# Narrowing 64-bit weights with one VectorE pass fewer and one ScalarE pass more, a group begun in halves, and new dates for a written schedule

## The chip, the cores and the metric

The kernel runs on one core of a Trainium2 chip. The metric is the device time of one execution in microseconds (us). Five engines work side by side, each in the order of its own queue: TensorE (PE in the profile), VectorE (DVE), ScalarE (ACT), GpSimd (POOL) and SyncE (SP), which here only starts DMAs. They wait for each other through semaphores.

## The reference

Two layers follow each other. The first is a recurrence over time with a complex decay, the second a gated feed-forward layer.

```python
# q, k, v, a_re, a_im: (4 batches, 8 heads, 768 steps, 48), float32
mag = sqrt(a_re * a_re + a_im * a_im)
scale = minimum(mag, 0.999) / (mag + 1e-06)
a_re_n, a_im_n = a_re * scale, a_im * scale
for t in range(S):
    new_re = ar * S_re - ai * S_im          # S: 48 x 48 for each batch and head
    new_im = ar * S_im + ai * S_re
    S_re, S_im = new_re + outer(k[t], v[t]), new_im
    y[t] = q[t] @ S_re
# x = y as (3072 tokens, 384); weights 384 x 1536, 384 x 1536, 1536 x 384
rms = sqrt(mean(x * x, axis=-1) + 1e-06)
xn = x / rms * rms_g
g = xn @ w_gate
out = (g * sigmoid(g) * (xn @ w_val)) @ w_out
```

The inputs of the first layer and `rms_g` are float32. The three weight matrices are divided by a square root from NumPy, and so they arrive as float64.

## The kernel before, in words

**Chunks, units and groups.** The 3072 tokens are cut into 24 chunks of 128 steps (`n`), six to a batch. `gates(u)` works out the decays of a unit: units 0 and 1 hold one chunk each, every later one holds two. Its stages are named "size", "root", "turn" and "rot": squares, roots and running products of the magnitudes, running sums of the angles, sines of them, and at the end q and k turned and scaled (`rot0`, `rot1`, `kin`). Six DMAs then lay the turned rows out for TensorE (`kq0`, `kq1`). `send_decays` sends the decay at the end of a chunk to the state: for units 0 and 1 by a small product on TensorE out of `ot1` and `ot0`, for the others by DMA. `attend(n)` makes the masked score products (`kq`, masked into `am` by VectorE), the outputs `y` in bank 6, the new state through bank 5 (`vn`, `kt`), and the norm: squares (`sq`), a column sum on TensorE (`ones`), `ssv` on VectorE, a power of -0.5 on GpSimd (`rs`), and that scale spread over 128 rows by a product with `ident`. The normed chunk goes to its half of `xT`. Two chunks are a group (`g`) for the feed-forward layer. Groups 0 to 2 are done by `feed`: six blocks `b`, each with two gate products of 256 columns into one bank and two value products into another, a Silu on ScalarE (`sg`), a product on VectorE (`hT`), and then the products with `wo`. Later groups go through `joint`, which shares products between forms of `x` and of the weights.

**The weights.** `pieces` cuts the float64 weights into twelve: pieces 0, 2 and 4 are the three thirds of `wg`, 1, 3 and 5 those of `wv` (1536 numbers to a partition each), and 6 to 11 are sixths of `wo` (768 numbers). `fetch` loads a piece by a DMA on GpSimd's queue into the room of `wo` or `hT`; a load waits for the one two pieces before it, seen by a copy of one element (`junk`), and piece 4 also for a copy (`seen`) of `kq1`. `narrow` then makes float32 out of the two words of each number. ScalarE scales the low word to its three top bits. VectorE shifts the high word left by three, puts sign and exponent right by a second pass, and adds the low bits by a third. The same weights are loaded once more later and looked at for numbers out of range (`look`); those loads are on SyncE's queue.

**The order.** Nothing is issued in the order of the code. Every call adds an operation to `Flow`, with an assumed duration, what it reads and writes (`box` gives the bytes), and a due time that follows from those that need it. `flow.shift` moves the due times of a stage by some microseconds. `schedule` picks for each engine the operation that is due first among those whose inputs it takes to be ready, by its own durations, and takes a DMA's time from its bytes and packets. `issue` then writes the instructions in that order. So a change of a duration or of a due time moves instructions on all engines. All instructions come from `issue` and therefore carry one line, L715 before and L716 after the change. `flow.warm` puts products that nobody reads (`bank3` out of `rot0`) where the planner expects TensorE to be idle early on.

## Time and profile before

| | us |
|---|---|
| median of three runs | 701.25 |
| lowest and highest of them | 699.18, 704.5 |
| the profiled execution | 701.28 |
| its span, first to last instruction | 699.5 |
| TensorE busy | 657.1 (94%) |
| VectorE busy | 559.4 (80%) |
| ScalarE busy | 477.9 (68%) |
| GpSimd busy | 59.7 (9%) |

The profiled execution is within 0.1 us of the median. Its span leaves 1.8 us outside the instructions. TensorE is nearly always busy, except at the beginning: its busy share in the first two of 40 slices of the span (17.5 us each) is 0 and 0.6, and part of that is products that nobody reads. The mean granted clock of TensorE is 0.989 of full speed.

Busy time of an engine is an average; what a change is worth has to be read at the place where the engine that sets the end waits. Since all of the kernel's instructions have one line number, groups are told apart by the names of their tiles and by their shapes.

### The profile page before, as it was taken

Reading aid. Unit: us, or ns where it says so; the run is one execution under the profiler, and the core shown is the slowest. Engines: PE = TensorE matmul, PEld = TensorE weight load, DVE = VectorE, ACT = ScalarE, POOL = GpSimd, SP = SyncE. Lnnn points to the kernel's source line nnn. Section 1 sums busy time; section 2 is a strip of 40 time slices with the busy share of each in tenths; the row PEclk is TensorE's granted clock in tenths of the full one; section 3 lists DMA queues with packets and bytes.
Section 4 is the critical chain, followed back from the end, with each engine's and each line's share of the span. In section 5 each row is a group of like instructions: output and inputs, shape, how many; then the busy total and the mean of one; then the engine's idle time right before and its main releaser. Section 6 shows DMA issues by size and latency. Waiting matters only on the chain.

```text
span 699.5 us, 18714 instructions
## 1 busy us (share of the span) xinstructions
PE 657.1 (94%) x7792; PEld 607.5 (87%) x7792; DVE 559.4 (80%) x1017; ACT 477.9 (68%) x807; POOL 59.7 (9%) x108
## 2 busy tenths in 40 slices
PE   0698999999999999999999999999999998999995
PEld 0587867886889999998999999999999998999995
DVE  8989888869888788888788889888898896356462
ACT  8657777898654675574675684675674884688884
POOL 3122100011000001000101010001000010000000
PEclk9989999999999999999999999999999999999999
DMA  9995462535424243434504334424623543834422
GB/s 292 291 290 178 154 166 75 148 65 106 111 57 103 60 82 62 134 77 86 128 17 80 96 70 96 126 60 86 133 53 75 119 97 112 250 94 145 149 72 91
DMA packets 104012, 81.98 MB, mean 117 GB/s; under 512 B 41936, under 2 KB 94416, under 8 KB 103920
## 3 DMA queue, kind: packets, MB, share of 16 engines
q1 hardware_dynamic: 98560, 64.78, 34.6%
q0 software_dynamic: 4416, 15.35, 10.3%
q8 instruction: 62, 1.02, 0.6%
q10 hardware_dynamic: 944, 0.59, 0.3%
q14 instruction: 30, 0.25, 0.1%
HBM read 55.84 MB, written 4.72 MB: 87 GB/s over the span
## 4 chain that ended last, share of the span: by engine, by line
PE 79%; DVE 7%; ACT 6%; DMA 3%; SPq 2%; issue 2%; POOL 0%; DVEq 0%; ACTq 0%
PE bank L715 79%; SPq L715 2%; DMA kq<-kin 2%; ACT turns L715 2%; ACT L715 1%; DVE hT L715 1%; DVE rot L715 1%; ACT t L715 1%; DVE wv L715 1%; DVE turns L715 1%; DMA in<-in_a_im_dram 1%; DVE wg L715 1%; DMA in<-in_a_re_dram 1%; DVE t L715 1%; DVE in L715 0%
## 5 line engine op out<-in xcount | busy, mean ns | idle before, releaser
L715 PE MATMUL bank<-wo,hT 128*128 128x192 f32 (+1 forms) x696 | 143.7, 352 | 0.9 <-DVE hT L715 0.9
L715 PEld LDWEIGHTS bank<-wo,hT 128*128 128x128 f32 x696 | 115.5, 191 | 13.3 <-DVE hT L715 1.8
L715 PE MATMUL bank<-xT,wg 128*128 128x128 f32 (+1 forms) x504 | 98.2, 330 | 0.0
L715 PE MATMUL bank<-xT,wv 128*128 128x128 f32 (+1 forms) x504 | 94.3, 321 | 0.0
L715 PEld LDWEIGHTS bank<-xT,wg 128*128 128x128 f32 x504 | 80.2, 194 | 7.4 <-issue 0.4
L715 PEld LDWEIGHTS bank<-xT,wv 128*128 128x128 f32 x504 | 79.1, 192 | 5.9 <-ACT turns L715 0.2
L715 ACT ACT_TABLE_LOAD x51 | 65.4, 1283 | 7.3 <-DVE t L715 2.8
L715 ACT ACTIVATE hT<-bank 128x512 f32<-128x512 f32 x90 | 52.4, 594 | 25.9 <-PE bank L715 23.1
L715 POOL TENSOR_TENSOR rs<-ssv,mhalf 128x1 f32<-128x1 f32 x24 | 20.6, 858 | 479.0 <-DVE ssv L715 428.3
L715 ACT ACTIVATE sg<-bank 128x512 f32<-128x512 f32 (+1 forms) x72 | 38.9, 540 | 21.1 <-PE bank L715 17.9
L715 DVE TENSOR_TENSOR hT<-hT 128x768 f32<-128x768 f32 (+1 forms) x58 | 50.5, 871 | 1.1
L715 ACT ACTIVATE bank<-bank 128x512 f32<-128x512 f32 x54 | 31.5, 583 | 26.8 <-PE bank L715 18.9
L715 ACT ACTIVATE kt<-bank 128x384 f32<-128x384 f32 x40 | 19.5, 489 | 43.9 <-PE bank L715 34.8
L715 DVE COPY_PREDICATED am<-causal,bank 128x512 f32<-128x512 int32 x48 | 34.7, 731 | 16.0 <-PE bank L715 15.9
L715 PE MATMUL bank<-yg,wg 128*128 128x128 f32 x288 | 45.7, 281 | 0.0
L715 PE MATMUL bank<-sums,hT 128*128 128x192 f32 x240 | 44.7, 328 | 0.1
L715 PE MATMUL bank<-yg,wv 128*128 128x128 f32 x288 | 43.9, 275 | 0.0
L715 DVE TENSOR_TENSOR hT<-bank,hT 128x512 f32<-128x512 f32 x45 | 30.9, 688 | 14.8 <-ACT bank L715 7.8
L715 PEld LDWEIGHTS bank<-kq 96*32 96x32 f32 x1536 | 31.3, 112 | 12.6 <-issue 4.5
L715 PE MATMUL bank<-kq 96*32 96x128 f32 (+3 forms) x1536 | 37.0, 240 | 5.4 <-DMA kq<-kin 3.6
L715 ACT ACTIVATE turns<-in 128x768 f32<-128x768 f32 (+1 forms) x39 | 30.4, 791 | 13.8 <-DVE kin L715 12.7
L715 PEld LDWEIGHTS bank<-sums,hT 128*128 128x128 f32 x240 | 39.3, 190 | 0.5 <-DVE yg L715 0.2
(216 smaller groups left out, 1417.4 us busy)
## 6 DMA issues: line engine op xcount, KB each, us to landing
kq<-rot SPq DMA_DIRECT2D x90, 128.0 KB, 2.5
kq<-kin SPq DMA_DIRECT2D x54, 128.0 KB, 2.7
kin<-in_q_dram SPq DMA_DIRECT2D x24, 192.0 KB, 3.2
kin<-in_k_dram SPq DMA_DIRECT2D x24, 192.0 KB, 3.4
out_dram<-ot SPq DMA_DIRECT2D x23, 192.0 KB, 2.8
in<-in_a_re_dram SPq DMA_DIRECT2D x11, 384.0 KB, 4.3
in<-in_a_im_dram SPq DMA_DIRECT2D x11, 384.0 KB, 4.2
vn<-in_v_dram SPq DMA_DIRECT2D x20, 192.0 KB, 2.6
```

Source lines behind the costliest of these rows:

```text
L715: fn(*args, **kw)
```

## The change

Six edits come together.

`narrow` does without the second VectorE pass. ScalarE now writes the low bits as a 16-bit number into the lower half of the low word, and by one more pass the sign of the number as a bfloat16 of plus or minus one into its upper half. VectorE shifts the high word and adds the low word. What comes out is half the weight. To make up for it, `gate_col` holds twice `rms_g` and `val_col` four times, the light units are scaled by `gate_col`, and `feed` doubles the outputs of the groups before the weights are scaled.

The planner's time for a byte of DMA goes from 50.3e-6 to 41e-6. In group 0, the first two blocks of `feed` are made in 128-column halves, one for each chunk. The sending of decays becomes a stage of its own, so that it can have its own date. The table of dates is a new one.

```diff
-        load = n / row * (0.006 + 50.3e-6 * row) / 16
+        load = n / row * (0.006 + 41e-6 * row) / 16
...
+    MORE = [1.0 if x.dtype == FP32 else 2.0 for x in (w_gate, w_val, w_out)]
+    act(gate_col, gcol, AF.Copy, scale=MORE[0])
+    act(val_col, gcol, AF.Copy, scale=MORE[1] * MORE[2])
...
         t = to.bitcast(I32)
-        act(lo, lo.bitcast(U32), AF.Copy, scale=2.0 ** -29)
-        step = n // 2 if i in HALVED else n
-        for f in range(0, n, step):
-            to_, lo_, hi_ = (x[:, :, f:f + step] for x in (t, lo, hi))
-            add("DVE", [(nc.vector.tensor_scalar, (),
-                         dict(out=to_, in0=hi_, scalar1=3, scalar2=None, op0=ALU.logical_shift_left))],
-                0.15 + 0.52e-3 * rows * step, [hi_], [to_])
-            stt(to_, hi_, 0x3FFFFFFF, to_, ALU.bitwise_or, ALU.bitwise_and)
-            tt(to_, to_, lo_, ALU.add)
+        low, high = (places[i].bitcast(d).rearrange("p (c f four) -> p c f four", f=n, four=4)[:, :, :, k]
+                     for d, k in ((U16, 0), (BF16, 1)))
+        act(low, lo.bitcast(U32), AF.Copy, scale=2.0 ** -29)
+        act(high, hi.bitcast(FP32), AF.Sign)
+        add("DVE", [(nc.vector.tensor_scalar, (),
+                     dict(out=t, in0=hi, scalar1=3, scalar2=None, op0=ALU.logical_shift_left))],
+            0.15 + 0.52e-3 * rows * n, [hi], [t])
+        tt(t, t, lo, ALU.add)
...
     def send_decays(u):
         ns = UNITS[u]
+        flow.stage = "decay", u
...
-                act(yg[:, j], yT[:, j], AF.Copy, scale=gcol[:, j:j + 1])
+                act(yg[:, j], yT[:, j], AF.Copy, scale=gate_col[:, j:j + 1])
...
+    SPLIT = 2
...
             for o, w_ in zip(ps, (wg, wv)):
+                if g == 0 and b < SPLIT:
+                    for t in range(2):
+                        list_ = []
+                        for i in range(2):
+                            f = b * 2 + i
+                            for d in range(ND):
+                                list_.append((o[:, i * T + t * C:i * T + (t + 1) * C],
+                                              w_[:, f // 4, d, f % 4 * P:(f % 4 + 1) * P],
+                                              xT[:, d, t * C:(t + 1) * C], d == 0, d == ND - 1))
+                        dur = 2 * ND * mm_time(C)
+                        clock[0] += dur * SPREAD
+                        mms(list_, dur, due=clock[0] - (1 - t) * dur)
+                    continue
...
-            act(ots[i], o, AF.Copy)
+            act(ots[i], o, AF.Copy, scale=MORE[2])
...
     flow.shift = {
-        ("attend", 8): 0.6, ("attend", 9): 3.8, ("attend", 11): 3.3, ("attend", 14): 1.6, ("attend", 15): -6.6,
...
+        ("attend", 11): 2.4, ("attend", 19): -0.6, ("attend", 20): -1.1, ("attend", 21): -1.7,
...
```

**What moves at the start.** The first place is VectorE's queue where the chunks 0 and 1 are turned. `rot` is the turned q and k, `wv` and `wg` with `wo` or `hT` behind the arrow are the passes of `narrow` (`TENSOR_SCALAR` the shift, `SCALAR_TENSOR_TENSOR` the pass that goes, `ISA` the add), and `ends` and `ot1` are what the small decay product of unit 1 needs. Before:

```order
L715 TENSOR_TENSOR rot0_105<-kin_100,turns_104 128x768 x2
L715 SCALAR_TENSOR_TENSOR in0_98<-turns_104 128x384
L715 TENSOR_SCALAR wv_92<-wo_93 128x1536
L715 SCALAR_TENSOR_TENSOR wv_92<-wo_93,wv_92 128x1536
L715 TENSOR_TENSOR turns_104<-turns_104,t2_102 128x2x384
L715 TENSOR_TENSOR rot1_106<-kin_100,turns_104 128x768 x2
L715 ISA wv_92<-wo_93,wv_92 128x3072
L715 TENSOR_SCALAR wg_91<-wo_93 128x1536
L715 SCALAR_TENSOR_TENSOR wg_91<-wo_93,wg_91 128x1536
L715 ISA wg_91<-wo_93,wg_91 128x3072
L715 TENSOR_TENSOR ends_83<-t4_103,t2_102 128x3
L715 TENSOR_TENSOR ot1_134<-ends_83,ot1_134 128x24
```

After, from the same place:

```order
L716 TENSOR_TENSOR rot0_107<-kin_102,turns_106 128x768 x2
L716 SCALAR_TENSOR_TENSOR in0_100<-turns_106 128x384
L716 COPY decay0_111<-bank0_65 96x8
L716 TENSOR_TENSOR ends_85<-t4_105,t2_104 128x3
L716 TENSOR_TENSOR ot1_136<-ends_85,ot1_136 128x24
L716 ISA wg_93<-wo_95,wg_93 128x3072
L716 TENSOR_TENSOR turns_106<-turns_106,t2_104 128x2x384
L716 TENSOR_TENSOR rot1_108<-kin_102,turns_106 128x768 x2
L716 COPY decay1_112<-bank1_66 96x8
L716 TENSOR_SCALAR wg_93<-hT_96 128x1536
```

`ends` and `ot1` now stand directly behind `rot0`, where two pieces of weights stood between them.

The second place is GpSimd's queue at the same time. `in_w_gate_dram` and `in_w_val_dram` are loads of weight pieces, `seen` are the copies that wait for `kq0` and `kq1`, and `rs` are the powers of the norm of chunks 0 and 1. Before:

```order
L715 DMA hT_94<-in_w_gate_dram 128x3x1024
L715 COPY junk_138<-hT_94 1x1
L715 DMA wo_93<-in_w_val_dram 128x3x1024
L715 COPY junk_138<-hT_94 1x1
L715 COPY seen_139<-kq0_107 96x1
L715 COPY junk_138<-wo_93 1x1
L715 TENSOR_TENSOR rs0_128<-ssv_127,mhalf_75 128x1
L715 COPY seen_139<-kq1_108 96x1
L715 DMA wo_93<-in_w_gate_dram 128x3x1024
L715 DMA hT_94<-in_w_out_dram 128x2x768
L715 TENSOR_TENSOR rs1_129<-ssv_127,mhalf_75 128x1
```

After:

```order
L716 DMA hT_96<-in_w_val_dram 128x3x1024
L716 COPY junk_140<-hT_96 1x1 x2
L716 COPY seen_141<-kq0_109 96x1
L716 COPY seen_141<-kq1_110 96x1
L716 DMA wo_95<-in_w_gate_dram 128x3x1024
L716 TENSOR_TENSOR rs0_130<-ssv_129,mhalf_75 128x1
L716 DMA wo_95<-in_w_val_dram 128x3x1024
L716 TENSOR_TENSOR rs1_131<-ssv_129,mhalf_75 128x1
```

The fifth weight load now stands behind the copy that sees `kq1` landed, where before it was issued ahead of both copies. A sixth load stands directly ahead of the second power.

The third place is TensorE's queue at the state of chunk 16 (`vn`, `kt`, into bank 5) and the scores of chunk 17 into the same bank (`kq0`). Before:

```order
L715 MATMUL bank3_68<-xT1_96,wg_91 128x128 x2
L715 MATMUL bank3_68<-xT1_96,wv_92 128x128 x2
L715 MATMUL bank5_70<-vn0_121,kt0_117 32x48 x24
L715 MATMUL bank5_70<-kq0_107 32x128
L715 MATMUL bank5_70<-kq0_107 32x96
```

After:

```order
L716 MATMUL bank5_70<-vn0_123,kt0_119 32x48 x24
L716 MATMUL bank4_69<-yg1_128,wg_93 128x128 x2
L716 MATMUL bank4_69<-yg1_128,wv_94 128x128 x2
L716 MATMUL bank1_66<-ve2_122,in1_101 128x128 x2
L716 MATMUL bank1_66<-ve2_122,kq1_110 128x128 x2
L716 MATMUL bank3_68<-yg0_127,wg_93 128x128 x2
L716 MATMUL bank3_68<-yg0_127,wv_94 128x128 x2
L716 MATMUL bank4_69<-xT1_98,wg_93 128x128 x2
L716 MATMUL bank4_69<-xT1_98,wv_94 128x128 x2
L716 MATMUL bank2_67<-xT1_98,wg_93 128x128 x2
```

Three more such pairs follow before the scores; before the change the scores came next after the state.

On TensorE's queue the half products of group 0 stand behind the product that spreads the norm of chunk 1 (`ident`, `rs1`), and both halves of a bank follow each other; 17 products that nobody reads stand ahead of the scores of chunk 0, where 40 did.

More of the change, by code (lines that the diff above doesn't have):

```diff
@@ L13 @@
 BF16 = mybir.dt.bfloat16
+U16 = mybir.dt.uint16
 AF = mybir.ActivationFunctionType
@@ L846, in dma @@
         op["load"] = load
-        op["packet"] = max(0.07, 0.006 + 50.3e-6 * row * (2 if eng == "POOL" and row == 2048 else 1))
+        op["packet"] = max(0.07, 0.006 + 41e-6 * row * (2 if eng == "POOL" and row == 2048 else 1))
         return op
@@ L1613, in fast @@
-        ("norm", 19): -0.1, ("norm", 20): -0.4, ("norm", 21): -1.4, ("norm", 22): -1.4, ("root", 0): -2.0,
-        ("root", 3): 21.5, ("root", 8): -10.8, ("rot", 2): -4.7, ("rot", 9): -1.1, ("scale", 0): 2.7,
-        ("size", 3): 2.2, ("size", 4): -9.6, ("size", 6): -8.3, ("size", 9): 14.4, ("size", 11): -1.5,
-        ("state", 2): -0.3, ("state", 4): -17.0, ("state", 6): -16.7, ("state", 8): -4.3, ("state", 13): -37.5,
-        ("state", 14): -11.8, ("state", 15): -8.0, ("state", 19): -14.7, ("state", 22): -0.3, ("turn", 9): 5.8,
[3 rows of a table removed]
+        ("attend", 11): 2.4, ("attend", 19): -0.6, ("attend", 20): -1.1, ("attend", 21): -1.7,
@@ new lines, in fast @@
+        ("attend", 22): -1.4, ("decay", 8): -3.5, ("decay", 9): -3.5, ("decay", 10): -1.9, ("decay", 11): -3.5,
+        ("decay", 12): -2.9, ("feed", 1): 29.9, ("feed", 2): 6.4, ("feed", 4): 11.9, ("feed", 5): 1.7,
+        ("feed", 7): 1.9, ("feed", 8): 2.1, ("feed", 9): 2.1, ("feed", 11): 2.0, ("form", 6): 3.3,
+        ("form", 7): 11.0, ("form", 8): 45.8, ("form", 9): 9.1, ("form", 10): 46.2, ("kq", 2): 6.1,
+        ("kq", 12): 13.9, ("load", 3): -24.3, ("look", 6): 48.5, ("look", 7): 26.1, ("look", 8): -0.2,
@@ new lines, in fast @@
+        ("look", 13): 60.0, ("look", 14): 66.3, ("look", 15): 61.0, ("look", 16): 18.1, ("norm", 5): 0.1,
+        ("norm", 11): 22.7, ("norm", 21): -1.3, ("root", 0): -1.9, ("root", 4): 11.3, ("root", 10): -21.1,
+        ("root", 11): 1.8, ("rot", 4): 26.8, ("rot", 5): 1.2, ("rot", 7): 30.5, ("rot", 10): 2.2,
+        ("rot", 12): -2.8, ("size", 4): -19.9, ("size", 5): -43.2, ("size", 9): 13.7, ("size", 10): -9.5,
+        ("size", 11): -7.5, ("state", 4): -13.8, ("state", 7): -42.4, ("state", 8): -2.0, ("state", 12): 9.6,
@@ L1621, in fast @@
+        ("state", 13): -16.4, ("state", 14): -7.6, ("state", 15): -8.3, ("state", 18): -8.1,
+        ("state", 19): -5.9, ("state", 20): -8.1, ("state", 21): -8.1, ("state", 22): 6.8, ("turn", 3): 9.4,
+        ("turn", 10): 0.2, ("turn", 11): -5.5, ("turn", 12): -12.8, ("w", 0): 4.7, ("w", 1): 62.1,
+        ("y", 6): -10.7, ("y", 14): 1.6, ("y", 16): -0.3, ("y", 18): 1.3, ("y", 21): -4.2, ("y", 23): -0.6,
     }
```

11 lines of the change are left out of this document (4 added, 7 removed), and 3 rows, old and new, of the table filler.

## The prediction

> **What bounds the kernel now.** First I read the busy time by stretches (us; busy and count of PE, PEld, DVE, ACT, POOL; then clock, DMA share, GB/s), for the time before and after the first real blocks of the feed-forward layer.
>
> ```profile
> 50.00:90.00 40.00, 37.42 (x216) 31.58 (x215) 36.88 (x49) 30.24 (x40) 8.09 (x12) 0.96 0.59 185
> 60.00:693.00 633.00, 624.58 (x7366) 577.89 (x7365) 505.11 (x933) 437.50 (x744) 42.87 (x67) 1.00 0.41 101
> ```
>
> From 60 us to the last product TensorE is busy 624.58 of 633.0 us. So from there on the kernel is TensorE's work, and only 8.4 us in it are idle. No edit takes TensorE's work away. What can be won is an earlier start of that work, and parts of the 8.4. So I asked next whom TensorE waits for (us in total, times, longest), and then for its queue in the first 60 us.
>
> ```profile
> PE bank L715 <- DVE ot L715: 20.0, 2, 17.0
> PE bank L715 <- DMA kq<-kin: 3.8, 3, 2.5
> PE bank L715 <- POOL rs L715: 2.9, 2, 2.3
> PE bank L715 <- DMA kq<-rot: 1.1, 1, 1.1
> PE bank L715 <- DVE state L715: 0.7, 1, 0.7
> PE bank L715 <- DMA vn<-in_v_dram: 0.4, 1, 0.4
> ```
>
> ```profile
> 22.32 10.09 PE L715 MATMUL bank<-rot 128*128 128x128 f32 x76 [4.24 <-DVE rot L715]
> 35.47 1.13 PE L715 MATMUL bank<-ot,ot 128*96 128x8 f32 x6 [3.06 <-DVE ot L715]
> 37.59 2.36 PE L715 MATMUL bank<-kq 96*32 96x128 f32 x64
> 42.66 0.85 PE L715 MATMUL bank<-vn,kt 128*32 128x48 f32 x48
> 44.83 1.33 PE L715 MATMUL bank<-kq 96*32 96x128 f32 x64
> 54.75 0.49 PE L715 MATMUL bank<-ident,rs 128*128 128x128 f32 x2 [2.25 <-POOL rs L715]
> 55.88 4.52 PE L715 MATMUL bank<-xT,wg 128*128 128x256 f32 x12
> 60.24 2.75 PE L715 MATMUL bank<-xT,wv 128*128 128x256 f32 x12
> 62.83 2.75 PE L715 MATMUL bank<-xT,wg 128*128 128x256 f32 x12
> 93.58 1.33 PE L715 MATMUL bank<-kq 96*32 96x128 f32 x64 [1.10 <-DMA kq<-rot]
> ```
>
> The scores of chunk 0 begin at 37.59, behind the decay product of unit 1, which waited for `ot` until 35.47. Group 0 begins at 55.88. VectorE tells why `ot` is late:
>
> ```profile
> 21.31 1.83 DVE L715 TENSOR_TENSOR rot<-kin,turns 128x768 f32<-128x768 f32 x2
> 24.51 1.76 DVE L715 SCALAR_TENSOR_TENSOR wv<-wo,wv 128x1536 int32<-128x1536 int32 x1
> 28.92 1.75 DVE L715 CUSTOM_DVE_ANT_0 wv<-wo,wv 128x3072 uint16<-128x3072 uint16 x1
> 35.24 0.18 DVE L715 TENSOR_TENSOR ot<-ends,ot 128x24 f32<-128x24 f32 x1
> 50.77 1.76 DVE L715 CUSTOM_DVE_ANT_0 wv<-wo,wv 128x3072 uint16<-128x3072 uint16 x1
> 52.45 0.15 DVE L715 TENSOR_SCALAR ssv<-bank 128x1 f32<-128x1 f32 x1
> ```
>
> The passes over weights stand between `rot` and `ot`. Were `ot` done, the scores would have to wait for `kq0` alone. Its six DMAs, and those of `kq1` (count, issue time in ns, first and last issue; then us to landing, least, median, most):
>
> ```profile
> L715 SPq DMA_DIRECT2D kq<-rot x6: 562/600/622, 22.3 to 25.5; - x6
> DMA to landing us min/median/max: 5.4/5.9/6.4
> ...
> L715 SPq DMA_DIRECT2D kq<-rot x6: 550/600/607, 29.4 to 32.6; - x6
> DMA to landing us min/median/max: 2.3/3.7/7.8
> ```
>
> The last issue of `kq0` (25.5) took the least time, 5.4, so `kq0` was there at 30.9, 6.7 us before its first use; `kq1` was at 32.6 + 7.8 = 40.4.
>
> **The weights, part by part.** The pass that goes costs 1.76 us for each of six pieces of 1536 and about 0.95 for each of six of 768; the pass that comes is a ScalarE pass like the one that is there.
>
> ```profile
> L715 DVE SCALAR_TENSOR_TENSOR wo<-hT,wo 128x768 int32<-128x768 int32 x4 | 3.8, 952 | 0.0
> L715 ACT ACTIVATE wo<-wo 128x1536 int32<-128x1536 uint32 x4 | 6.5, 1624 | 0.0
> L715 ACT ACTIVATE hT<-hT 128x768 int32<-128x768 uint32 x4 | 3.6, 911 | 3.2 <-DMA hT<-in_w_out_dram 3.2
> ```
>
> VectorE is spared 6 x 1.76 + 6 x 0.95 = 16.3 us, all before about 110 us. ScalarE gets 6 x 1.62 + 6 x 0.91 = 15.2 us. The trace has no sign pass; I bound it by twice the 0.91 of a small pass, 1.8, from above, and by the shortest large one, 1.57 (next fence), from below, and take the mean of its likes, 1.6. Half a microsecond either way at the first of them would move the start by as much. The order puts no table load beside it. None of this is TensorE's time; what counts is where it stands.
>
> ```profile
> 14.81 1.57 ACT L715 ACTIVATE wo<-wo 128x1536 int32<-128x1536 uint32 x1
> 17.42 0.52 ACT L715 ACTIVATE turns<-in 128x384 f32<-128x384 f32 x1
> ```
>
> **The start, step by step.** The first sign pass stands ahead of the `turns<-in` of 17.42, from about 16.7 to 18.25. That puts the sines, and so `rot0`, 0.8 us later: it ends at 23.9, not 23.1. The six issues then begin at 23.1. The landing of `kq0` hung on a weight load in flight until about 28, and not on the issue alone, so I take 31.5 (bounds 30.9 and 31.7, both from the row of `kq0`). `ot` comes right behind `rot0`, at about 24.8. So the scores begin at 31.5, not 37.59: 6.1 us won.
>
> From there to the state (`vn`, `kt`) it was 42.66 - 37.59 = 5.1 us, and that took 0.8: 37.4. Next stand the scores of chunk 1, which follow at once if `kq1` is there. Its DMAs begin as before, at 29.4, but the weight load that was issued beside them at 31.23 now stands behind the copy that sees `kq1`. So I give the last of them the 2.3 of the first, not 7.8: landed near 35, before 37.4. (With the 7.8 it would be 40.4, and the start 3 us less.) From these scores to `ssv` of chunk 1 it was 52.45 - 44.83 = 7.6 us. The last 0.9 of that was a wait behind the add of 50.77, and an add stands there again. New are a sign pass ahead of the squares of chunk 0 and the masking of chunk 1 behind a shift. I take 8.1: `ssv` at 45.5.
>
> ```profile
> 31.23 0.78 POOL L715 DMA_DIRECT2D wo<-in_w_val_dram  x1 [8.05 <-DVE wv L715]
> 52.69 2.00 POOL L715 TENSOR_TENSOR rs<-ssv,mhalf 128x1 f32<-128x1 f32 x1 [3.70 <-DVE ssv L715]
> ```
>
> On GpSimd a weight load (0.8) now stands ahead of the power (2.0) of chunk 1. It waits for the same add as `ssv`, and starts just before: the load to 46.2, the power to 48.2. Spreading it and starting group 0 took 55.88 - 54.75 = 1.1; a half of the products needs only chunk 0, so I take 0.4 from the power on: group 0 begins at 48.6 instead of 55.88, 7.3 us earlier. Its bounds are 4 (`kq1` late as above, 3.3 less) and 8.5 (the load and the 0.4 hidden).
>
> **The halves.** They cannot begin before chunk 1's norm is spread, because they stand behind it; what they save is 0.7 of the 1.1 us above. They cost little: four such products take 0.45 us, twelve of 256 columns 2.59 (60.24 to 62.83).
>
> ```profile
> 344.10 0.61 PE L715 MATMUL bank<-ve,wg 128*128 128x128 f32 x4
> 344.55 0.61 PE L715 MATMUL bank<-ve,wv 128*128 128x128 f32 x4
> ```
>
> Four banks of 24 at 0.112 instead of 12 at 0.216 are 10.75 for 10.37: 0.4 us lost. The start is worth 6.9.
>
> **Group 0 to chunk 2.** The start is only kept if ScalarE keeps up, since its queue now holds 8.7 us more (two sign passes of 1.6, six of 0.91) in the 40 us where it was busy for 30.24. On an average it fits, with 1.1 us to spare. TensorE asks for rows 4 to 7 of `wo` behind twelve blocks of 2.59, the 1.8 of clock below, the 0.4 of the halves and one block with `wo` of 2.7: at 48.6 + 36.0 = 84.6. If ScalarE is never idle from group 0 on, the passes that stand ahead of those rows in its queue (my own adding up from rows like the above) end by 81, VectorE's by 82. Two or three microseconds is all the cover there is; each beyond them costs TensorE one. VectorE, with one pass fewer for each of the eight pieces left, turns chunk 2 earlier, so the wait of 1.1 at 93.58 goes. The state of chunk 1 now stands ahead of group 0 and frees `vn`, so the 0.4 goes too.
>
> **The dates.** The 0.7 behind the state at 454 goes, since twelve pairs of products now stand between the state of chunk 16 and the scores of chunk 17. Of the 8.4 that leaves 6.2, 3.8 of them for `kq<-kin`. For those I see no reason for fewer or for more, and leave the sum as it is, 4 us either way. The planner's price of a DMA has no cost of its own.
>
> A wait can also cost clock:
>
> ```profile
> 36.00:38.00 2.00, 2.00 (x21) 1.77 (x23) 1.65 (x3) 0.00 (x0) 0.00 (x0) 0.50 1.02 377
> 56.00:58.00 2.00, 2.00 (x5) 1.64 (x6) 1.97 (x2) 1.97 (x3) 0.81 (x2) 0.50 1.00 141
> 581.00:585.00 4.00, 4.00 (x45) 3.83 (x46) 0.52 (x1) 1.15 (x2) 0.00 (x0) 0.57 0.20 76
> ```
>
> After each of three idle stretches (3.06 and 2.25 above; 2.5, the longest for `kq<-kin`) TensorE ran at half clock. The first block of group 0 took 4.36 us to the next, not 2.59: 1.8 us. I keep all three, since the gap ahead of the scores (fillers end near 28, `kq0` at 31.5) and the one ahead of group 0 stay. The Trainium skill, in "TensorE: Matmul & The Clock Gate" (Part 1), says that the clock is halved after an idle window of about 3.4 us, and that the window runs free of the kernel. By that rule a gap of 2.3 us halves it only if other gaps share its window; the trace's 2.25 and 2.5 were followed by it. If one stretch escaped by it, the time would be 690.4.
>
> **The sum.** 6.9 + 1.1 + 0.4 + 0.7 = 9.1 us from 701.28, the profiled execution, which is the median to 0.1: 692.2.
>
> **The rivals.** *More than that (0.20).* The dates also remove most of the other 6.2 us of waits and a half-clock stretch of 1.8: about 685. For it: three of these waits are for DMAs, the longest 2.5 us. Against: nothing in the order aims at them.
> *Less than that (0.23).* Only the 4 of the lower bound arrive, as sign passes delay masks, sums and sines one after another on ScalarE, and new waits take back what the dates spare: about 697 (701.28 - 4).
> *Slower (0.07).* The planner now believes in faster DMAs, and so sends `kq` later for the 18 chunks from 6 on. The longest stall of that kind took 2.5, and 1.8 of clock. With four such stalls more than now (17 us) the kernel is at 709, over 1% slower; fewer leave it below. Against: among 18 chunks there was one so long.
> *The halves do nothing* (within the forecast, since the order says as much): if chunk 1 is waited for all the same, the 0.7 goes, and the time is 692.9.
>
> **The numbers.** The forecast (0.50) gives 692, and by its own bounds 688.5 to 696. About 1%, 7 us, is what a measurement of this kernel can tell from no change; the line is 694.2. Four fifths of the forecast and all of the first rival lie below: 0.40 + 0.20 = 0.60. The rest of the forecast and most of the second lie between: 0.33. Slower keeps 0.07. A range from 685 to 699 leaves out about a tenth on each side.
>
> **What would show it.** Scores of chunk 0 near 31.5 and group 0 near 48.6 on TensorE; `ot` right behind `rot0`; `kq1` landed by 36; no wait for `kq<-rot` at chunk 2; idle time of TensorE behind group 0 near 6 us. The forecast is wrong if group 0 begins after 52, if TensorE waits for `hT` or `sg` inside group 0, or if the waits for `kq<-kin` add up to more than 8.

## The result, and the profile after

The changed kernel took 724.48 us (median of 4 runs, 721.85 to 725.85), the kernel before, run beside it, 702.68 (699.18 to 704.5): a ratio of 1.031, with a 95% interval of 1.026 to 1.037. It is 3.1% slower, where 692 was forecast. Medians and ranges here and below are of all executions, and every ratio is of those within 1.5% of their kernel's fastest alone. The profiled execution took 723.73 us, with a span of 722.0, 22.5 longer than the 699.5 of before.

First the groups of instructions on ScalarE in the changed kernel (busy us, mean ns of one, idle before).

```profile
L716 ACT ACTIVATE wo<-wo 128x1536 uint16<-128x1536 uint32 x4 | 14.7, 3663 | 0.0
L716 ACT ACTIVATE wo<-wo 128x1536 bf16<-128x1536 f32 x4 | 14.6, 3661 | 0.1
...
L716 ACT ACTIVATE hT<-hT 128x768 bf16<-128x768 f32 x4 | 7.7, 1927 | 0.1
L716 ACT ACTIVATE hT<-hT 128x768 uint16<-128x768 uint32 x4 | 7.7, 1914 | 0.0
```

A large pass takes 3.66 us and a small one 1.92, and this holds for the sign pass and for the low pass alike. The low pass was there before, with the same input, and took 1.62 and 0.91; what changed in it is its output, from int32 to uint16. All 24 passes are 67.0 us of ScalarE, against 15.4 before. Next, ScalarE's timeline ahead of the first `rot`, the end of that `rot` on VectorE, and TensorE up to group 0.

```profile
15.41 3.59 ACT L716 ACTIVATE wo<-wo 128x1536 uint16<-128x1536 uint32 x1
18.75 0.57 ACT L716 ACTIVATE turns<-turns 128x384 int32<-128x384 f32 x1
19.23 3.61 ACT L716 ACTIVATE wo<-wo 128x1536 bf16<-128x1536 f32 x1
22.59 0.57 ACT L716 ACTIVATE turns<-in 128x384 f32<-128x384 f32 x1
```

```profile
25.53 0.96 DVE L716 TENSOR_TENSOR turns<-turns,t 128x768 f32<-128x768 f32 x1 [3.19 <-ACT turns L716]
26.52 1.83 DVE L716 TENSOR_TENSOR rot<-kin,turns 128x768 f32<-128x768 f32 x2
```

```profile
35.88 1.33 PE L716 MATMUL bank<-kq 96*32 96x128 f32 x64
...
44.78 1.42 PE L716 MATMUL bank<-vn,kt 128*32 128x48 f32 x45 [5.69 <-ACT kt L716]
...
60.26 2.84 PE L716 MATMUL bank<-xT,wg 128*128 128x128 f32 x24
...
79.50 4.54 PE L716 MATMUL bank<-xT,wg 128*128 128x256 f32 x12 [2.19 <-ACT sg L716]
...
90.36 4.44 PE L716 MATMUL bank<-xT,wg 128*128 128x256 f32 x12 [3.72 <-ACT sg L716]
94.64 2.75 PE L716 MATMUL bank<-xT,wv 128*128 128x256 f32 x12
```

Two narrow passes stand ahead of the sines, so `rot` ends at 28.3 instead of 23.1. The copies of `kt` queue behind more of them, and the state of chunk 0 waits 5.69 us for one. Group 0 begins 4.4 us later than before (60.26 for 55.88), and inside it TensorE waits for `sg`. Last, the busy time by stretches (PE, PEld, DVE, ACT, POOL; clock, DMA share, GB/s).

```profile
60.00:100.00 40.00, 33.22 (x183) 28.85 (x183) 26.38 (x36) 39.69 (x30) 5.93 (x9) 0.91 0.45 139
60.00:715.00 655.00, 632.70 (x7380) 583.20 (x7379) 506.92 (x934) 470.51 (x757) 45.89 (x71) 0.99 0.42 103
```

ScalarE is busy for 39.69 of the 40 us from 60 on, and TensorE is idle for 6.8 of them. From 60 us to the last product TensorE is idle for 22.3 us, against 8.4. So of the 22.5 us, 4.4 are the later start and 13.9 more idle time. Of the other 4.2, 1.5 is clock. Added up in stretches of 1 us from group 0 on (busy time times one less the clock), half speed costs 4.9 us here, most of it at 79.50 and 90.36, where a block takes 4.38 and 4.28 us to the next one instead of 2.59; in the kernel before it costs 3.4. Where the last 2.7 are from is not shown.

### The profile page after: what moved, and what is told of

It reads as the page before. It is cut to its first block, busy times and chain, and to the rows that moved or that the text cites. A ratio compares the mean times of both kernels' runs of the same rounds, so it can differ in the third digit from the quotient of the medians.

```text
span 722.0 us, 18705 instructions
## 1 busy us (share of the span) xinstructions
PE 659.4 (91%) x7786; PEld 607.5 (84%) x7786; DVE 545.3 (76%) x1005; ACT 525.3 (73%) x819; POOL 58.9 (8%) x108
## 4 chain that ended last, share of the span: by engine, by line
PE 67%; ACT 18%; DMA 5%; DVE 4%; SPq 3%; issue 2%; DVEq 0%; ACTq 0%
PE bank L716 67%; ACT hT L716 4%; ACT wo L716 4%; SPq L716 3%; ACT turns L716 2%; ACT L716 2%; ACT t L716 2%; DMA kq<-kin 2%; DMA in<-in_a_re_dram 1%; DVE hT L716 1%; ACT in L716 1%; ACT sg L716 1%; DVE turns L716 1%; DMA in<-in_w_gate_dram 1%; DMA kin<-in_k_dram 1%
## 5 line engine op out<-in xcount | busy, mean ns | idle before, releaser
L716 PE MATMUL bank<-xT,wg 128*128 128x128 f32 (+1 forms) x528 | 100.4, 327 | 9.2 <-ACT sg L716 9.1
L716 ACT ACTIVATE bank<-bank 128x512 f32<-128x512 f32 x54 | 31.5, 584 | 30.1 <-PE bank L716 25.3
L716 PEld LDWEIGHTS bank<-kq 96*32 96x32 f32 x1536 | 31.5, 112 | 10.7 <-issue 4.3
L716 PEld LDWEIGHTS bank<-yg,wg 128*128 128x128 f32 x288 | 38.0, 191 | 2.9 <-ACT hT L716 2.1
L716 PE MATMUL bank<-kq 96*32 96x96 f32 (+3 forms) x1536 | 37.3, 240 | 3.1 <-DMA kq<-kin 1.8
L716 PE MATMUL bank<-am,ve 128*32 128x128 f32 x768 | 39.0, 286 | 0.0
```

The costliest lines, as they stand in the source:

```text
L716: fn(*args, **kw)
```

## Theories

A: an output of 16 bit in every fourth place (8 bytes apart) is what makes a ScalarE pass slow, and the loss is that time. Rivals on the price: B, the sign function or reading fp32 is slow; C, writing in place; D, something that runs beside the passes. Rivals on the loss: E, the new dates, the DMA rate or the halves cost it; and A2, the passes could be hidden, had the planner known their price.

## The price of a pass, alone

Sixteen passes behind the last work of the kernel before:

```diff
+    steps = [
+        (words(A32, I32, 0, 2), lo32, AF.Copy),
+        (words(A32, U16, 0, 4), lo32, AF.Copy),
+        (words(A32, BF16, 1, 4), hi32, AF.Sign),
+        (words(A32, FP32, 0, 2), hi32, AF.Sign),
+        (words(B32, BF16, 0, 4), hi32, AF.Sign),
+        (words(B32, BF16, 0, 2)[:, 0:1536], hi32, AF.Sign),
+        (B32.bitcast(BF16)[:, 0:1536], hi32, AF.Sign),
+        (B32[:, 0:1536], hi32, AF.Sign),
+    ]
```

> The kernel before, with sixteen ScalarE passes over 1536 numbers per partition behind its last work, in rooms that are no longer read: two rounds of eight forms. (1) low word to int32, 8 bytes apart, in place; (2) the same to uint16, 8 bytes apart, in place; (3) Sign of fp32 to bf16, 8 bytes apart, in place; (4) Sign to fp32, 8 bytes apart, in place; (5) Sign to bf16, 8 bytes apart, into another room; (6) to bf16, 4 bytes apart; (7) to bf16, dense; (8) to fp32, dense. Nothing is left out; only the durations of these passes are wanted. Theory A (a 16-bit output is what is slow, at whatever place): forms 2, 3, 5 take 3.6 us, forms 1, 4, 8 take 1.6; whether 6 and 7 take 3.6 or 1.6 tells if the stride belongs to it. Theory B (Sign, or reading fp32, is slow): forms 3 to 8 all take 3.6, form 2 takes 1.6. Theory C (writing into the words that are being read is slow with the new layout): forms 2 and 3 take 3.6, form 5 takes 1.6. Theory D (what runs beside the passes in the first 100 us makes them slow): all eight take about 1.6 here, where nothing else runs.

The view of one tile in narrow stretches gives them nearly one by one (least, median, most, in ns; first and last start; forms).

```profile
L716 ACT ACTIVATE hT<-hT x2: 1592/2594/3596, 692.0 to 693.6; 128x1536 int32<-128x1536 uint32 x1, 128x1536 uint16<-128x1536 uint32 x1
L716 ACT ACTIVATE hT<-hT x2: 1547/2571/3595, 697.3 to 700.9; 128x1536 bf16<-128x1536 f32 x1, 128x1536 f32<-128x1536 f32 x1
L716 ACT ACTIVATE hT<-hT x2: 1547/2563/3579, 700.9 to 702.4; 128x1536 f32<-128x1536 f32 x1, 128x1536 bf16<-128x1536 f32 x1
L716 ACT ACTIVATE hT<-hT x2: 1561/1736/1911, 706.0 to 707.9; 128x1536 bf16<-128x1536 f32 x2
```

In order, forms 1 to 8 took 1.59, 3.60, 3.60, 1.55, 3.58, 1.91, 1.56 and (1581 ns in the same view) 1.58 us. Sign to fp32 costs what the copy to int32 costs, so B falls. Form 5 writes elsewhere and is as slow, so C falls. From 694 us on no other engine had work left, so D falls. The stride belongs to it: bfloat16 8 bytes apart takes 3.58, 4 bytes apart 1.91, dense 1.56. A stands, in the narrower form that 16-bit words 8 bytes apart cost 2.3 times as much as 32-bit words 8 bytes apart. The Trainium skill, in "ScalarE: Activation LUTs" (What ACT_TABLE_LOAD costs), gives an ACTIVATE with immediate scale and bias 186 ns and 0.833 ns for each element of a partition, fp32 and bf16 alike; by that figure all eight would take an estimated 1.47 us. The dense forms come near it, bfloat16 4 bytes apart takes 0.4 us more, the narrow ones 8 bytes apart are far off, and the measurement decides.

## What the price costs the kernel

The same two passes with 32-bit outputs. The order of all engines stays the changed kernel's, instruction for instruction, so this is the width alone.

```diff
...
-        act(low, lo.bitcast(U32), AF.Copy, scale=2.0 ** -29)
-        act(high, hi.bitcast(FP32), AF.Sign)
+        act(lo, lo.bitcast(U32), AF.Copy, scale=2.0 ** -29)
+        act(lo.bitcast(FP32), hi.bitcast(FP32), AF.Sign)
```

> The changed kernel, with the two ScalarE passes writing 32-bit words: the low pass int32, as before the change, and then the sign pass fp32 over the same words. The low pass's result is overwritten, so the three lowest bits of each weight are left out; the number of passes, their inputs and everything else is as in the changed kernel. Theory A (the 16-bit outputs are the loss): the passes take 1.6 us (1536) and 0.9 (768), group 0 begins near 49, and the time is near the 692 of the prediction, 688 to 698. Theory B (Sign is slow in itself): the low pass goes back to 1.6, the sign pass keeps 3.66, about half of the loss stays, 705 to 715. Theory E (the new dates, the DMA rate or the halves are the loss): the time stays at 720 to 726 whatever the passes take.

It took 708.62 us (ratio to before 1.007, 1.001 to 1.012). Twelve further runs of the same kernel are below (706.65). ScalarE's rows and TensorE's timeline:

```profile
L716 ACT ACTIVATE wo<-wo 128x1536 f32<-128x1536 f32 x4 | 6.6, 1652 | 0.1
L716 ACT ACTIVATE wo<-wo 128x1536 int32<-128x1536 uint32 x4 | 6.4, 1609 | 0.0
```

```profile
31.83 1.59 PE L716 MATMUL bank<-kq 96*32 96x128 f32 x64
...
48.43 0.88 PE L716 MATMUL bank<-vn,kt 128*32 128x48 f32 x48 [1.18 <-DMA vn<-in_v_dram]
...
50.05 4.21 PE L716 MATMUL bank<-xT,wg 128*128 128x128 f32 x24
...
91.31 2.36 PE L716 MATMUL bank<-kq 96*32 96x128 f32 x64 [3.12 <-DMA kq<-rot]
...
126.71 0.52 PE L716 MATMUL bank<-ident,kq 96*128 96x96 f32 x4 [1.89 <-DMA kq<-rot]
...
511.12 1.22 PE L716 MATMUL bank<-xT,wg 128*128 128x128 f32 x4 [2.87 <-ACT sg L716]
```

So the width is 16 of the 22 us, which is A. But A also expected the predicted 692 (688 to 698) here, and that did not come. The start did: scores of chunk 0 at 31.83 and group 0 at 50.05, 5.8 us before the old one. It is given back later, at waits that the kernel before did not have. This is taken up below.

With only the low pass widened (nothing is left out, and the order is again the changed kernel's):

```diff
-        act(low, lo.bitcast(U32), AF.Copy, scale=2.0 ** -29)
+        act(lo, lo.bitcast(U32), AF.Copy, scale=2.0 ** -29)
```

> The changed kernel, its order kept, with only the low pass widened: it writes the number 0 to 8 as int32 over the low word, and the sign pass then writes its bf16 into the upper half of it. The result is bit for bit that of the changed kernel; of the two ScalarE passes one has a 16-bit output. Theory A: low passes of 1.6 and 0.9 us, sign passes of 3.66 and 1.92, about half of the 16 us between 724.5 and 708.6 gone: 713 to 719. Theory A3 (the first narrow pass is covered by other work and only the second costs): below 711 or above 721.

It took 709.43 us (703.38 to 717.35; ratio 1.008, 1.004 to 1.013). That is A3's number: the loss isn't proportional. Widening the low passes alone won 15 of the 16 us, and group 0 began at 52.07; one wait for `sg` of 3.9 us was left in it. From the kernel with 32-bit outputs to this one ScalarE gets 18 us more and the time rises by 1 to 3; from this one to the changed kernel it gets 18 us more again, and the time rises by 15. The first fit beside the other work, and the second do not.

Next, the planner is told the price:

```diff
-        act(low, lo.bitcast(U32), AF.Copy, scale=2.0 ** -29)
-        act(high, hi.bitcast(FP32), AF.Sign)
+        act(low, lo.bitcast(U32), AF.Copy, scale=2.0 ** -29)["dur"] = 0.2 + 2.27e-3 * rows * n
+        act(high, hi.bitcast(FP32), AF.Sign)["dur"] = 0.2 + 2.27e-3 * rows * n
```

> The changed kernel with one thing different: the planner is told what the 16-bit ScalarE passes take (0.2 us plus 2.27 ns an element in place of 0.86), so it makes another order for the same instructions and the same dates. Theory A1 (the passes themselves are the loss, ScalarE has 52 us more in the first 120 us than it can hide): the time stays within a few us of the changed kernel's, 715 to 730. Theory A2 (the passes could be hidden, and the loss is an order made with too low a price): 700 to 710, and TensorE does not wait for ScalarE inside group 0.

Neither: 749.17 us (ratio 1.069). TensorE now waits 12.2 us at once for `kq` of a chunk, and 10.4 in all for `sg`:

```profile
PE bank L716 <- DMA kq<-rot: 12.9, 2, 12.2
PE bank L716 <- ACT sg L716: 10.4, 3, 6.0
```

A2 is not borne out. A truer price makes another order, with the same dates, and a worse one. Whether other dates could hide the passes at that price is not shown.

## The parts apart

The narrowing of before (one ScalarE pass, three VectorE passes, no factor of 2) with the new dates, rate and halves:

```diff
-    MORE = [1.0 if x.dtype == FP32 else 2.0 for x in (w_gate, w_val, w_out)]
+    MORE = [1.0 for x in (w_gate, w_val, w_out)]
...
-        act(low, lo.bitcast(U32), AF.Copy, scale=2.0 ** -29)
-        act(high, hi.bitcast(FP32), AF.Sign)
+        act(lo, lo.bitcast(U32), AF.Copy, scale=2.0 ** -29)
...
+        stt(t, hi, 0x3FFFFFFF, t, ALU.bitwise_or, ALU.bitwise_and)
         tt(t, t, lo, ALU.add)
```

> The changed kernel with the narrowing of before (one ScalarE pass, three VectorE passes, no factor of 2): dates, DMA rate and halves alone. Theory A: nothing here is slow by itself; VectorE has 16 us more than these dates were made for, ScalarE has 52 us less than the changed kernel, so the time is near that of before, 697 to 708. Theory E: the loss is here, 715 or more.

720.45 us (ratio 1.027, 1.023 to 1.032): E's number. TensorE waits in group 0 for a piece of `wv`, since VectorE has the third pass again and the new dates leave it no room (it is busy for 20.4 of the 21 us from 53 to 74):

```profile
74.02 4.21 PE L716 MATMUL bank<-xT,wv 128*128 128x128 f32 x18 [8.98 <-DVE wv L716]
```

The kernel before with the new narrowing alone (with it go the scales by `gate_col`, `val_col` and `MORE`, as in the change; no date, rate or half is touched):

```diff
-            stt(to_, hi_, 0x3FFFFFFF, to_, ALU.bitwise_or, ALU.bitwise_and)
-            tt(to_, to_, lo_, ALU.add)
...
+        act(low, lo.bitcast(U32), AF.Copy, scale=2.0 ** -29)
+        act(high, hi.bitcast(FP32), AF.Sign)
...
+        tt(t, t, lo, ALU.add)
```

> The kernel before with the new narrowing alone (two ScalarE passes with 16-bit outputs, two VectorE passes, the factor of 2 made good): old dates, old DMA rate, no halves. Theory A: the passes take 3.66 and 1.92 us here too, and the time is 715 to 735. Theory E: 695 to 705, the passes cost little.

726.98 us (ratio 1.036), as A had it. The same with 32-bit outputs:

```diff
-        act(low, lo.bitcast(U32), AF.Copy, scale=2.0 ** -29)
-        act(high, hi.bitcast(FP32), AF.Sign)
+        act(lo, lo.bitcast(U32), AF.Copy, scale=2.0 ** -29)
+        act(lo.bitcast(FP32), hi.bitcast(FP32), AF.Sign)
```

> The kernel before with the new narrowing, but 32-bit words from both ScalarE passes (the low pass's result is overwritten, so the three lowest bits of each weight are left out): old dates, old DMA rate, no halves. Against the run of the new narrowing alone at 726.98 it differs in the width of the outputs, against the run with 32-bit outputs and the new dates at 708.62 in dates, rate and halves. Theory A: about 18 us below 726.98, 705 to 712, since 36 passes of 16 bit cost that much there too. Theory E2 (beside the width, the new dates and the DMA rate cost the other part of the loss, by late loads of kq and of the inputs): clearly below 708.62, 695 to 703. Theory F (what is left of the loss is an order that the dates do not fit, whichever dates): 703 to 712.

704.57 us (697.77 to 708.53; ratio 1.001, 0.996 to 1.006). The width costs 22 us here, a few more than the 18 of A. The time fits F; it is just below A's 705 to 712 and above E2's 695 to 703. Group 0 begins at 58.16 there, no earlier than with the old narrowing. So one VectorE pass less and one ScalarE pass more win nothing with the old dates. The last way to spare VectorE, with no ScalarE pass more:

```diff
-        act(lo, lo.bitcast(U32), AF.Copy, scale=2.0 ** -29)
...
-            stt(to_, hi_, 0x3FFFFFFF, to_, ALU.bitwise_or, ALU.bitwise_and)
-            tt(to_, to_, lo_, ALU.add)
+        act(lo, lo.bitcast(U32), AF.Copy, scale=2.0 ** -29 * (1 - 2.0 ** -20), bias=-0.5)
+        stt(t, hi, 3, lo, ALU.logical_shift_left, ALU.bitwise_or)
+        stt(t, hi, 0x3FFFFFFF, t, ALU.bitwise_or, ALU.bitwise_and)
```

> The kernel before with VectorE's three passes made two without a ScalarE pass more: ScalarE gives the top three bits of the low word as int32, cut off instead of rounded, and VectorE shifts and ors them in one pass and masks in a second (the add goes). Old dates. The weights differ in their last bit at most. VectorE is spared 0.95 us for each of six large pieces and 0.55 for each of six small ones, 9 us in all, and ScalarE does as much as before. Theory A: with ScalarE as before the time is that of before or a few us lower, 695 to 702. Theory F: the order is made anew with dates that were fitted to another one, 702 to 715.

703.0 us (ratio 1.000, 0.996 to 1.003). VectorE's 9 us are worth nothing measurable in the total, though group 0 began 1.5 us earlier, at 54.39. The medians side by side (us):

| narrowing | old dates, old rate | new dates, new rate, halves |
|---|---|---|
| three VectorE passes | 702.2 | 720.5 |
| two, 16-bit outputs | 727.0 | 724.5 |
| two, 32-bit outputs | 704.6 | 708.6, again 706.7 |

With three VectorE passes the new dates, rate and halves lose 18 us. With 16-bit outputs they win 2.5, and with 32-bit outputs they lose 2 to 4, but there the intervals of the ratios overlap (1.026 to 1.037 and 1.032 to 1.040; 1.001 to 1.012 or 0.997 to 1.007, and 0.996 to 1.006). The parts do not add up: each alone costs 18 and 25 us, both together 22. The halves and the table of dates were not run alone.

## Where the earlier start went

In the kernel with 32-bit outputs the stretches 80 to 100 and 500 to 600 look like this, the kernel before below it:

```profile
80.00:100.00 20.00, 16.88 (x155) 12.02 (x157) 13.77 (x21) 13.65 (x18) 0.76 (x3) 0.83 0.83 187
500.00:600.00 100.00, 94.48 (x1249) 89.99 (x1249) 79.73 (x150) 65.56 (x118) 7.79 (x11) 0.95 0.38 87
```

```profile
80.00:100.00 20.00, 18.90 (x272) 15.15 (x271) 17.25 (x25) 12.37 (x18) 2.65 (x4) 1.00 0.56 160
500.00:600.00 100.00, 97.31 (x1329) 93.75 (x1328) 82.75 (x161) 68.10 (x124) 5.81 (x9) 0.98 0.43 100
```

Idle time plus the busy time that half clock cost (busy times one less the clock) is 6.0 us against 1.1 in the first stretch and 10.2 against 4.6 in the second. Two late loads stand behind it. At 91.31 the scores of chunk 2 wait for `kq`, whose DMAs run beside the last two loads of the output weights (DMA share 0.83). At 511.12 TensorE waits for `sg`, which ScalarE makes behind a pass that waits for `in_a_re` of unit 12:

```profile
509.74 0.84 ACT L716 ACTIVATE t<-in 128x768 f32<-128x768 f32 x1 [3.47 <-DMA in<-in_a_re_dram]
510.49 0.58 ACT L716 ACTIVATE sg<-bank 128x512 f32<-128x512 f32 x1
```

First `kq`. The row of its landing, in that kernel and then with those two loads cut to a quarter:

```profile
L716 SPq DMA_DIRECT2D kq<-rot x12: 551/596/1097, 76.8 to 88.2; - x12
...
DMA to landing us min/median/max: 6.5/8.4/11.1
```

```profile
L716 SPq DMA_DIRECT2D kq<-rot x12: 550/598/1547, 78.2 to 87.3; - x12
...
DMA to landing us min/median/max: 2.4/3.4/4.6
```

The cut, put in behind the planning, so that the order stays:

```diff
     flow.schedule()
+    for i in (10, 11):
+        load_ = next(o for o in flow.ops if o["stage"] == ("w", i) and o["land"] is not None)
+        fn, args, kw = load_["calls"][0]
+        f = kw["in_"].shape[-1] // 4
+        load_["calls"] = [(fn, args, dict(out=kw["out"][..., 0:f], in_=kw["in_"][..., 0:f]))]
```

> The kernel with 32-bit outputs (708.62), its order kept, and the transfers of the last two pieces of the output weights cut to a quarter (three quarters of two of the twelve weight pieces are left out, and the three lowest bits of all weights; every instruction stays). In that kernel the twelve DMAs of kq for chunks 2 and 3, from 76.8 on, took 6.5 to 11.1 us to land while those two loads of 768 KB ran; TensorE waited 3.1 us for kq at 91.3 and then ran at half clock for a block and the scores. Theory G (kq is late because it shares the DMA engines with the weight loads, which the planner takes for faster than they are): kq lands in 3 to 6 us, the wait at 91 goes with its half clock, 5 to 6 us less, 702 to 704. Theory H (kq is late because VectorE finishes rot late, at 81.6): the wait shrinks by less than 1 us, 706 to 709.

702.09 us (698.54 to 704.64; ratio 0.999, 0.996 to 1.003): G. By the ratios the gain over the kernel without the cut is 2 to 5 us (1.002 in the further runs below, 1.007 above), so the total alone would not show it. TensorE no longer waits for `kq` of chunk 2, and from 80 to 100 it is never idle. H falls: the twelve issues came at much the same time (78.2 to 87.3), and the wait went.

The other late load was moved:

```diff
     flow.schedule()
+    late_ = next(o for o in flow.ops if o["stage"] == ("load", 12))
+    last_ = [o for o in flow.ops if o["stage"] == ("rot", 10) and o["eng"] == "SP"][-1]
+    late_["order"] = last_["order"] + 0.25
```

> The kernel with 32-bit outputs (708.62; three lowest bits of each weight left out), its order kept instruction for instruction, and one DMA issue moved: the load of in_a_re for unit 12, which was issued at 503.9 behind nine other DMAs of SyncE's queue and for which ScalarE, with a copy to sg behind it, waited until 509.7. It now stands ahead of those nine. Theory G (the new order has single late loads, each costing TensorE its wait and then half clock): the 2.9 us of waiting at 508 and the half clock up to 517, about 2.5, go: 5 us less, 702 to 705. Theory H (TensorE waits for something else there too, or loses the same at the next place): 706 to 710.

In the trace the wait at 511 is gone with its half clock (idle and clock cost 2.6 us from 500 to 600, not 10.2). The median, 707.46 (697.04 to 713.39; ratio 0.999, 0.994 to 1.005), does not show it. In the profiled execution the state of chunk 1 waited 3.14 us for `vn` instead of 1.18, and group 0 began at 53.59; the start itself moves by a few microseconds from one execution to the next. By its total this run settles nothing. Both mended, and the kernel with neither, on the same chip:

> The kernel with 32-bit outputs, order kept, with both late loads mended: the load of in_a_re for unit 12 moved ahead, and the last two pieces of the output weights cut to a quarter (three quarters of two of the twelve pieces are left out, and the three lowest bits of all weights). Theory G: TensorE waits neither at 91 nor at 508, 9 to 11 us less than the same kernel without the two edits: 696 to 700. Theory H: as with the cut alone, 700 to 703.

> The kernel with 32-bit outputs once more, unchanged, beside the run with both loads mended: three of its four times were 708 to 709 and one 701.7. Theory G: most times stay at 706 to 709, median above 705. If the median is below 704, what the two edits won before was within the scatter of single executions.

698.66 us with both (692.89 to 702.9; ratio to before 0.995, 0.991 to 0.998), 706.65 with neither (697.95 to 714.95; ratio 1.002, 0.997 to 1.007). In the trace with both mended TensorE waits at neither place. By the medians the two late loads are worth 8 us, by the ratios 5, with intervals that just touch; the 9 to 11 of G was more than either. So that these loads cost time is shown by the traces, and how much only roughly. The unmended kernel scatters by 17 us. Its second profiled execution took 699.87: there the same two waits were 1.5 and 1.8 us, and no half clock followed them:

```profile
90.30 1.33 PE L716 MATMUL bank<-kq 96*32 96x128 f32 x64 [1.48 <-DMA kq<-rot]
...
506.09 0.71 PE L716 MATMUL bank<-xT,wg 128*128 128x128 f32 x4 [1.79 <-ACT sg L716]
```

Beside 3.12 and 2.87 us in the first one, each followed by products at half speed (2.36 and 1.22 us for what takes 1.33 and 0.71 here), these two places make most of the difference between the two executions, whose spans are 8.4 us apart: 2.7 us of waiting and about 6 of half clock, against a group 0 that began 1.6 us later in the faster one (51.65). The other executions have no trace, so what their scatter is from is not shown.

Why the loads were late: the planner takes DMAs for faster. That edit alone, in the kernel before:

```diff
-        load = n / row * (0.006 + 50.3e-6 * row) / 16
+        load = n / row * (0.006 + 41e-6 * row) / 16
...
-        op["packet"] = max(0.07, 0.006 + 50.3e-6 * row * (2 if eng == "POOL" and row == 2048 else 1))
+        op["packet"] = max(0.07, 0.006 + 41e-6 * row * (2 if eng == "POOL" and row == 2048 else 1))
```

> The kernel before with one edit: the planner takes DMAs to be faster (41e-6 in place of 50.3e-6). No instruction is added or left out. Theory E2 (believing in faster DMAs makes loads late): 706 to 715, with waits of TensorE for kq. Theory F (any new order with the same dates loses a little): 702 to 708. No effect: 699 to 703.

712.89 us (ratio 1.015, 1.009 to 1.022): the time that E2 had. The scores of chunk 0 come early, at 30.64, and those of chunk 1 then wait 8.4 us. The view names another DMA of the same queue; of the six of `kq1`, issued from 29.4 on, the slowest took 11.1 us to land.

```profile
30.64 1.33 PE L715 MATMUL bank<-kq 96*32 96x128 f32 x64 [1.01 <-DMA ve<-in_v_dram]
...
43.75 2.36 PE L715 MATMUL bank<-kq 96*32 96x128 f32 x64 [8.40 <-DMA in<-in_a_im_dram]
```

The old rate put back in the kernel with 32-bit outputs:

```diff
-        load = n / row * (0.006 + 41e-6 * row) / 16
+        load = n / row * (0.006 + 50.3e-6 * row) / 16
...
-        op["packet"] = max(0.07, 0.006 + 41e-6 * row * (2 if eng == "POOL" and row == 2048 else 1))
+        op["packet"] = max(0.07, 0.006 + 50.3e-6 * row * (2 if eng == "POOL" and row == 2048 else 1))
```

> The kernel with 32-bit outputs and the new dates (708.62), with the old DMA rate put back in the planner; again the three lowest bits of each weight are left out. Theory E2 (the faster DMAs that the planner believes in make loads late: kq of chunk 2 cost 3.1 us of waiting, an input load at 508 made TensorE wait 2.9, and each was followed by half clock): these two waits go, 695 to 702. Theory F (dates fit one order only, and any other price makes another order with other waits): the waits go to other places, 703 to 715.

709.33 us (ratio 1.010, 1.003 to 1.017), F. The two waits named are nearly gone (0.86 us for `kq` at 95.74, 0.4 at 512), but group 0 begins at 56.13 instead of 50.05. The rate brings the earlier start and the late loads together.

Two tries for a version faster than both. The low pass left out, with the order kept:

```diff
     flow.schedule()
+    for o in flow.ops:
+        if o["eng"] == "ACT" and o["stage"] and o["stage"][0] == "w" and o["calls"][0][2].get("scale") == 2.0 ** -29:
+            o["calls"] = []
```

> The kernel with 32-bit outputs, its order kept, without the low pass on ScalarE: one ScalarE pass and two VectorE passes for a piece, so ScalarE has as much to do as before the change and VectorE 16 us less (the three lowest bits of each weight are left out, as in the kernel with 32-bit outputs). Theory K (ScalarE's additional passes of 1.6 us still delay the start and the blocks of group 0): rot of chunk 0 ends 1.6 us earlier, group 0 begins near 48.5, and the time is 704 to 706. Theory G (what is lost behind group 0 hangs on the late loads and not on ScalarE): the start is gained at most and lost again at kq of chunk 2, 706 to 710.

And with that two DMA issues moved, the load for unit 12 as above and a load of q:

```diff
+    late_ = next(o for o in flow.ops if o["stage"] == ("kq", 3) and o["eng"] == "SP")
+    last_ = [o for o in flow.ops if o["stage"] == ("rot", 2) and o["eng"] == "SP" and o["land"] is not None]
+    late_["order"] = max(o["order"] for o in last_) + 0.25
```

> The kernel of one ScalarE pass with the order kept, the load of in_a_re for unit 12 moved ahead as above, and the load of q for unit 3 moved behind the second six DMAs of kq, in whose way it stood at 80.8 (the three lowest bits of each weight are left out). Theory G: both late loads are mended, the first for 5 us, the second for about 1 us plus its half clock: 699 to 702, a little faster than the kernel before. Theory H: 704 to 710.

702.56 us (700.57 to 710.45; ratio 1.001, 0.997 to 1.005) and 705.44 (698.08 to 711.49; ratio 1.003, 0.999 to 1.007); before, beside both, 702.15. The first is below what either theory had, though its profiled execution had a later start than the kernel with both passes (group 0 at 55.34, behind a wait of 6.2 us for `kq0`). By the ratios it is not a clear gain over that kernel (1.001 beside 1.007 and 1.002). The second was as fast as G's 699 to 702 in its profiled execution (698.76) and not in the median. No version that computes the whole beat the kernel before.

## Why the prediction was wrong, point by point

**The step that failed first is the price of the passes.** "The pass that comes is a ScalarE pass like the one that is there" set 1.6 us, with 1.57 and 1.8 as bounds. It is 3.66. I compared passes by their element count and left the type of the output out, and so I also kept the old price for the low pass, whose output the diff changes to uint16. ScalarE got 51.6 us, not 15.2. With the measured price the next steps work: the low pass 2.0 longer and a sign pass of 3.4 put `rot0` at 23.1 + 5.4 = 28.5, and 28.3 was measured. The same holds for the limit that I gave for group 0, two or three microseconds of cover: it was passed, and TensorE waited for `sg`, as the last part said it would if the forecast was wrong.

**The start, at the price that I took, was right.** With 32-bit outputs `rot0` ended at 24.1 (23.9 predicted), the scores came at 31.83 (31.5 predicted) and group 0 at 50.05 (48.6 predicted), 1.2 of it a wait for `vn` that I had not counted. One step on the way met its time by luck: the scores of chunk 1 came at 37.34, where 37.4 follows from the prediction, but the state ahead of them was done at 36.0, earlier than I had it, and they then waited 1.37 us for `kq1`, which I had landed near 35.

**The second step that failed is "leave the sum as it is" for the waits behind the start,** with "the planner's price of a DMA has no cost of its own". In that kernel the earlier start of 5.8 us was given back at late loads and the half clock behind them. I had chunk 2's wait for `kq` going away since VectorE turns earlier. It came, since the DMAs of `kq` now ran beside the loads of the output weights. Had the passes cost 1.6 us, the forecast would still have been 15 us too low (medians of 706.7 and 708.6 for 692; by the ratios, 1.002 and 1.007, it is 10 to 14). And the new rate alone cost 9.8 us (712.89 against 703.05 of the kernel before beside it).

**The rivals.** *Slower* had the right sign, with 0.07, and named the DMA rate, which does cost when it stands alone. Its place was wrong: waits for `kq<-kin` were 2.3 us in all, less than before. *Less than that* had the mechanism of the first 120 us, ScalarE's passes delaying what stands behind them, but set its price so that 4 us were still won.

**Right:** the wait behind the state of chunk 16 went; the halves cost 0.1 us for each of four banks, 2.68 for 2.59; `ot` came right behind `rot0` (29.0 behind 28.3); no table load was added (49 for 51). The clock agreed with the rows used: the long waits, 2.19 and 3.72 us for `sg`, were followed by blocks at half speed.

## What to carry to other kernels

Price an added instruction by a row of the same output type and stride, not by the same element count, and look at old instructions whose output type the edit changes; where no such row is there, the upper bound is open. Dates belong to the instructions and prices that they were set for: the new narrowing, the new dates with rate and halves, and the new rate each lost when taken alone. An earlier start is worth what the loads behind it allow, so ask of every load that comes earlier what it will share the DMA engines with.

## What the runs showed of the hardware

ScalarE took 3.60 us to write 1536 16-bit words per partition 8 bytes apart, 1.91 at 4 bytes apart and 1.56 side by side, and 1.55 to 1.59 for 32-bit words 8 bytes apart; copying uint32 or taking the sign of fp32, in place or not, made no difference. Waits of TensorE that differ by one or two microseconds differed by more in the total. At the same two places of one order 2.9 and 3.1 us were followed by half clock, and 1.5 and 1.8 were not. The length alone does not decide: in both executions a wait of 1.89 us (at 126.71 in the first) was followed by half clock, its next block taking 4.0 us for 2.6, and 2.25 us was followed by it in the kernel before and not with only the low pass widened. Twelve transfers of `kq` took 6.5 to 11.1 us to land beside two large loads, and 2.4 to 4.6 with these loads cut to a quarter.
